# Adding two more key tiles of P on GpSimd before the row sums, and writing the last rows of maxima late in the burst

## The chip, the cores and the metric

The kernel runs on one core of one Trainium2 chip. The metric is device time in microseconds (us), the median of three runs. A profile was taken of one further execution; its times are counted from the start of its span. The engines are called PE (TensorE), DVE (VectorE), ACT (ScalarE), POOL (GpSimd) and SP (SyncE); PEld is the loading of PE's stationary operand.

## What is computed

The reference is an attention whose mask comes from a clustering of queries and keys, followed by two blocks of dense layers:

```
mask   = argmax(q_n . c_n)[:, :, :, None] == argmax(k_n . c_n)[:, :, None, :]
scores = where(mask, scale * q @ k.T, -1e9);  scores -= max(scores)
attn   = exp(scores);  attn /= (sum(attn) + 1e-9)
x      = attn @ v                                   # 2 batches, 8 heads, 768 rows, 64 wide
u      = x + (w_tok_r @ (x cos(x w_theta)) + w_tok_i @ (x sin(x w_theta)))
x      = u + relu(u @ w_ch)
u      = x + (x.T @ U @ V).T
out    = u + relu(u @ w_ch1) @ w_ch2
```

The change touches the attention alone: the sum of `attn` over the keys, and the place of a step that brings the row maxima into the operand of the scores.

## The kernel before

The attention works on 8 groups (`g` = 0 to 7), each two heads (`h` = 0, 1) of one batch. The scores are kept transposed: P, the exponentials, has keys on the partitions, in 6 key tiles of 128 keys by 768 queries in single precision (`pt[g, h, kt]`). Every engine works through its own queue in the order in which the program issues; nothing is reordered between instructions of one engine. That order is written out by hand in `attention()`: a loop over groups, and in it a loop over 6 slots, `p` = 0 to 5.

A slot of a middle group does this, in this order of the program:

- `scores_pair` (L304, L309): the scores of two key tiles by PE, their exponentials by ACT. Head 0 has slots 0 to 2, head 1 slots 3 to 5.
- `max_pair` (L251, L255): the plain scores of two query tiles of the next group by PE, their maxima by DVE straight from PSUM. Behind slot 2 and slot 5, `max_join` takes the last maximum (DVE, L260) and `max_split` splits it into two bf16 parts on POOL: a cast (L271) and a subtraction (L272).
- `join_keys` (L332) adds key tiles 0 and 1 of P into a tile `pj`. In groups 0 to 3 POOL does it (slots 1 and 4), in groups 4 to 6 DVE (slots 2 and 4). `join_third` (L340) adds key tile 2 on POOL, in groups 1 to 3 (slots 2 and 5).
- `split_half` (slots 0 and 1) has POOL subtractions L193; `row_sums` of the group before (end of slot 2) has a DVE reciprocal (L367) and eight small POOL copies (L373).
- `fill` runs background work whose costs the program keeps account of: parts of the clustering (`assign_items`, L124 to L152), the normalisation of the group before (`spread` L379, `norm_x` L383, DVE), and the conversion of weights (`Convert`: ACT L407 and L419, DVE L410 and L414, POOL L423).

Slot 5 of groups 1 to 6 ends in what is called the burst here: the clustering's `sims`, the rows of maxima of head 0 for the next group (`max_rows`: six small PE matmuls L282 of the split maxima, and two ACT copies L285 into the operand `qp`), about 9.6 us worth of background work, the products P times V (`pv`, L317, each of 8 PE instructions) and, between them, the rows of maxima of head 1, and at the end `sum_keys` (L354): matmuls of ones with each tile that is left, which sum P over the keys. In groups 1 to 5 twelve `pv` stand in the burst, in group 6 six (the other six go into group 7). `sum_keys` has 8 PE instructions for each key tile of both heads, so that adding tiles together beforehand makes it shorter. Its sums go to DVE (L357) and into `row_sums` of the next group.

After the attention come the dense layers (`mixer`), from 227 us to the end.

Of the kernel before, what the change touches and what calls it, by code (L numbers as in the profile page):

```python
# [16 lines left out]
ALU = mybir.AluOpType  # L17
# [7 lines left out]
NG = B * NP  # L25
# [16 lines left out]
def tile_cluster_block(ctx: ExitStack, tc: tile.TileContext, qk, v, cent, wth, wr, wi, wch,  # L42
                       u_in, v_in, w1, w2, cst, out):
    nc = tc.nc
# [7 lines left out]
    def slot(name, dt=F32, shape=None):  # L52
        return sp.tile(shape or [P, S], dt, tag="slot", name=name)
# [5 lines left out]
    def bank(name, keep=None):  # L59
        i = ring.popleft()  # L60
        if keep is None:
            ring.append(i)
        else:
            kept.setdefault(keep, []).append(i)
        return pp.tile([P, 512], F32, tag=f"bank{i}", name=name)
# [34 lines left out]
    def load_raw(g, i):  # L100
        t = slot(f"raw{g}_{i}")
        nc.sync.dma_start(out=t, in_=qk[g // NP, g % NP, i])
        raw[g, i] = t
# [8 lines left out]
    def cols(hf):  # L112
        return slice(hf * HALF, (hf + 1) * HALF)
# [174 lines left out]
    pt, v_t, pvt, xT = {}, {}, {}, {}  # L288

    def load_v(g):  # L290
        t = slot(f"v{g}", F32, [P, NT, P])
        nc.sync.dma_start(out=t, in_=v[g // NP, g % NP])
        v_t[g] = t
# [19 lines left out]
    def pv(g, kt, hf):  # L313
        if kt == 0 and hf == 0:
            pvt[g] = banks("pv", "pv")
        for r in range(0, P, 32):
            nc.tensor.matmul(out=pvt[g][hf][r:r + 32, :HALF], lhsT=v_t[g][:, kt, r:r + 32],  # L317
                             rhs=pt[g, r // 64, kt][:, cols(hf)],
                             start=(kt == 0), stop=(kt == NT - 1))

    def pv_out(g):
        xT[g] = slot(f"xT{g}")
        for hf in range(2):
            nc.scalar.activation(out=xT[g][:, cols(hf)], in_=pvt[g][hf][:, :HALF], func=AF.Copy)
        give("pv")

    rl, lsum, joined = {}, {}, {}
# [4 lines left out]
        eng.tensor_tensor(t, pt[g, h, 0], pt[g, h, 1], op=ALU.add)  # L332
        joined[g, h] = t

    wide = set()

    def join_third(g, h):

        t = joined[g, h]
        nc.gpsimd.tensor_tensor(t, t, pt[g, h, 2], op=ALU.add)  # L340
        wide.add(g)

    def sum_keys(g, a, n=3):

        ps = bank("l")
        x = [[pt[g, h, kt] for kt in range(3 * a, 3 * a + n)] for h in range(2)]
        if (g, 1) in joined and a == 0:
            x = [[joined.pop((g, h)), *x[h][3 if g in wide else 2:]] for h in range(2)]
        n = len(x[0])
        for i in range(n):  # L350
            for h in range(2):
                for hf in range(2):
                    o = 32 * (2 * h + hf)
                    nc.tensor.matmul(out=ps[o:o + 32, :HALF], lhsT=ones, rhs=x[h][i][:, cols(hf)],  # L354
                                     start=(i == 0), stop=(i == n - 1))
        lt = slot("lt")[:, :HALF]
        nc.vector.transpose(lt, ps[:, :HALF])  # L357
        lsum[g, a] = lt
# [76 lines left out]
    def conv_start():  # L435
        while conv_load and len(conv_in) < STAGED:
            c = conv_load.popleft()
            c.load()
            c.at = clock[0]
            conv_in.append(c)  # L440
# [30 lines left out]
    def weigh_in(src, n, dst):  # L471
        return [Convert(src, n, i, keep_split(dst)) for i in range((n + S - 1) // S)]
# [378 lines left out]
    def split_half(g, i):  # L851
        split_hi(g, i)
        split_lo(g, i, nc.gpsimd)
        if i:
            pack(g)

    def attention():


        ORDER = [(0, 0), (0, 2), (0, 4), (1, 0), (1, 2), (1, 4)]  # L860
        BURST = (2, 5)
        pvq = deque()
        held[0] = True

        def next_pv():
            g, kt, hf = pvq.popleft()
            pv(g, kt, hf)
            if kt == NT - 1 and hf:
                pv_out(g)

        for g in range(NG):
            nxt = g + 1 < NG
            if g == 1:
                conv_load.extend(weigh_in(wth, NP * DM, wth_t))
                conv_start()
            if nxt:
                load_v(g + 1)
            if g < 2:
                bg.extend(assign.pop(g + 2))
            if g + 3 < NG:  # L880
                for i in range(2):
                    load_raw(g + 3, i)
            if g == 2:
                tok = [c for p in zip(weigh_in(wr, NT * S, wr_t), weigh_in(wi, NT * S, wi_t)) for c in p]
                conv_load.extend(tok[:6])
                conv_start()
                late = tok[6:]
            if g == 5:
                conv_load.extend(late)
                conv_start()  # L890
            if not nxt:
                for t in range(NP):
                    bg.append((1., lambda t=t: split_x(0, t, nc.gpsimd)))
            order = [(1, 0), None, (1, 2), None, (1, 4), None] if g == 0 else ORDER
            for p in range(NT):
                ready = len(pvq)
                clock[0] = NT * g + p
                if order[p]:
                    h, a = order[p]
                    scores_pair(g, h, a)  # L900
                    if h:
                        pvq.extend((g, kt, hf) for kt in (a, a + 1) for hf in range(2))
                if g == 0 and p < 2:
                    mask_direct(1, p, nc.scalar if p else nc.vector)
                if nxt:
                    max_pair(g + 1, p // 3, 2 * p % 6)
                    if p % 3 == 2:
                        max_join(g + 1, p // 3)

                while conv_after:  # L910
                    conv_after.popleft()()
                if p in ((1, 4) if g < 4 or not nxt else (2, 4)):
                    join_keys(g, p // 4, nc.gpsimd if g < 4 else nc.vector)
                    if 4 <= g < NG - 1 and p == 4:
                        owed[0] -= .95
                if 0 < g < 4 and p in (2, 5):
                    join_third(g, p // 5)
                if p < 2 and g + 2 < NG:
                    split_half(g + 2, p)
                if p == (3 if g < 2 else 2) and g + 2 < NG:  # L920
                    mask_rows(g + 2)
                long = 0 < g < NG - 1 and p == 5
                if long:
                    if g + 3 < NG:
                        (_, sims), *items = assign_items(g + 3)
                        sims()
                        bg.extend(items)
                    max_rows(g + 1, 0)
                if g > 0 and p == 5:
                    bg.appendleft((.95, lambda: norm_x(g - 1)))  # L930
                    bg.appendleft((.97, lambda: spread(g - 1)))
                fill(2.5 if not nxt else .3 if p not in BURST or (g > 1 and p == 2) else 9.6 if g > 1 else 4.8)
                if not nxt:
                    for _ in range(min(ready, (2, 2, 2, 0, 4, 4)[p])):
                        next_pv()
                    if p == 5:
                        sum_keys(g, 0)
                elif long:
                    ready = len(pvq) - (6 if g == NG - 2 else 0)
                    for n in range(ready):  # L940
                        if n == ready // 2:
                            max_rows(g + 1, 1)
                        next_pv()
                    sum_keys(g, 0, NT)
                elif p == 2 and g < 2:
                    if g > 0:
                        max_rows(g, 1)
                        sum_keys(g - 1, 1)
                    for _ in range(min(ready, 6)):
                        next_pv()  # L950
                elif p == 5:
                    max_rows(g + 1, 0)
                    for _ in range(min(ready, 6)):
                        next_pv()
                    sum_keys(g, 0)
                    (_, sims), *assign[g + 3] = assign_items(g + 3)
                    sims()
                if g > 0 and p == 2:
                    row_sums(g - 1)
            while bg:  # L960
                fill(.5)
            while g and conv_after:
                conv_after.popleft()()
        held[0] = False
        while len(pvq) > 1:
            next_pv()
        nc.scalar.activation(out=warm, in_=warm, func=AF.Sin)
        next_pv()
        sum_keys(NG - 1, 1)
# [286 lines left out]
```

## Time and profile before

| | |
|---|---|
| runs | 671.27, 668.59, 669.45 us; median 669.45 us |
| profiled execution | 670.76 us, of which the span of instructions is 669.0 us |
| busy, share of the span | PE 98%, PEld 87%, DVE 69%, ACT 54%, POOL 49% |
| chain that ended last | PE 91%, DVE 5%, POOL 1%, ACT 1% |
| mean granted TensorE clock | 0.994 of full speed |

A matmul's end is modelled in the profile, so PE's busy share is no measure of what it could do; idle time of PE, and what ended it, can be read as it stands. A merged row of the timeline gives start, length, engine, line, operation, tiles (written from read), sizes and count, and in brackets the idle time of the engine ahead of it with what ended that. An instruction's row begins when its engine takes it up, so a row longer than its like holds a wait inside the engine.

### The profile page before, as it was taken

What the parts mean: (1) busy time and instruction counts of PE and PEld (TensorE: products, weight loads), DVE (VectorE), ACT (ScalarE), POOL (GpSimd) and SP (SyncE); (2) the same over time, 40 slices, a digit from 0 to 9 for tenths busy, and PEclk for the clock granted to TensorE, in tenths of its full rate; (3) what the DMA queues carried; (4) which work ended last, traced back from release to release, by engine and by line L of the source; (5) the groups of instructions that cost most, each with busy time, mean ns of one, the idle gap of its engine ahead of it and who ended that gap; (6) DMA issues with size and microseconds to landing.
All of it is one profiled execution on the core that took longest, in us unless ns stands there. A gap on an engine that the chain in (4) does not pass through costs nothing.

```text
span 669.0 us, 11891 instructions
## 1 busy us (share of the span) xinstructions
PE 656.9 (98%) x4535; PEld 579.6 (87%) x4536; DVE 463.8 (69%) x795; ACT 359.1 (54%) x726; POOL 325.7 (49%) x331
## 2 busy tenths in 40 slices
PE   8899999999999999999999999999999999999998
PEld 3566787777665699999999998889999999999997
DVE  6888699897799466457374556769876576766554
ACT  8657487667679454555455446634553444533231
POOL 9445296534329433113233144967766564746221
PEclk9799999999999999999999999999999999999999
DMA  6867677695715111003101221113221122110013
GB/s 201 219 145 249 159 172 233 177 228 157 215 35 169 62 48 33 0 18 99 45 23 33 78 70 43 32 32 95 63 80 51 61 79 79 32 33 1 0 48 142
DMA packets 21786, 62.57 MB, mean 94 GB/s; under 512 B 4224, under 2 KB 7296, under 8 KB 21728
## 3 DMA queue, kind: packets, MB, share of 16 engines
q1 hardware_dynamic: 21728, 61.80, 32.2%
q8 instruction: 36, 0.59, 0.4%
q14 instruction: 22, 0.18, 0.1%
HBM read 40.35 MB, written 3.15 MB: 65 GB/s over the span
## 4 chain that ended last, share of the span: by engine, by line
PE 91%; DVE 5%; POOL 1%; ACT 1%; issue 0%; DMA 0%; SPq 0%; POOLq 0%; DVEq 0%
PE acc L824 17%; PE q L772 15%; PE y L590 15%; PE st L304 9%; PE pv L317 9%; PE h L610 5%; PE th L548 5%; PE smax L251 4%; PE l L354 3%; DVE mx L255 3%; PE g L726 3%; PE acc L745 3%; PE tp L628 1%; PE th L552 1%; PE sims L121 1%; PE h L672 0%
## 5 line engine op out<-in xcount | busy, mean ns | idle before, releaser
L824 PE MATMUL acc<-g,wh 128*128 128x384 f32 x448 | 113.7, 334 | 0.0
L786 POOL TENSOR_TENSOR g<-sum,g 128x384 fp32r<-128x384 f32 x56 | 61.8, 1105 | 83.5 <-ACT g L785 83.5
L255 DVE TENSOR_REDUCE mx<-smax 128x1 f32<-128x512 f32 x144 | 89.0, 679 | 10.9 <-PE smax L251 10.8
L780 DVE TENSOR_TENSOR xT<-acc,xT 128x384 f32<-128x384 f32 x112 | 61.9, 554 | 46.4 <-PE acc L824 46.3
L309 ACT ACTIVATE p<-st 128x512 f32<-128x512 f32 x192 | 80.2, 519 | 24.3 <-PE st L304 23.9
L590 PE MATMUL y<-wh,z 128*128 128x384 f32 x384 | 87.6, 340 | 0.3 <-ACT z L568 0.3
L824 PEld LDWEIGHTS acc<-g,wh 128*128 128x128 f32 x448 | 80.9, 188 | 0.1
L304 PE MATMUL st<-qp,kp 128*128 128x256 f32 (+1 forms) x384 | 80.0, 351 | 0.5 <-ACT qp L285 0.2
L423 POOL TENSOR_TENSOR wl<-cv,wh 128x768 fp32r<-128x768 f32 (+1 forms) x31 | 56.5, 1829 | 40.0 <-ACT wh L419 39.7
L824 PE MATMUL acc<-g,wl 128*128 128x384 f32 x224 | 74.8, 334 | 0.0
L304 PEld LDWEIGHTS st<-qp,kp 128*128 128x128 f32 x384 | 58.6, 193 | 17.4 <-issue 7.2
L784 ACT ACTIVATE sum<-sum 128x384 f32<-128x384 f32 x56 | 29.3, 523 | 82.3 <-DVE sum L780 82.3
L780 DVE TENSOR_TENSOR sum<-q,sum 128x384 f32<-128x384 f32 x98 | 53.0, 553 | 24.4 <-PE q L772 20.8
L590 PEld LDWEIGHTS y<-wh,z 128*128 128x128 f32 x384 | 66.9, 188 | 0.5 <-ACT z L568 0.5
L317 PE MATMUL pv<-p,v 128*32 128x384 f32 x768 | 66.6, 487 | 0.0
L574 POOL TENSOR_TENSOR z<-tht,z 128x256 fp32r<-128x256 f32 x24 | 18.6, 774 | 90.8 <-ACT z L568 90.7
L317 PEld LDWEIGHTS pv<-p,v 128*32 128x32 f32 x768 | 38.9, 110 | 18.7 <-issue 8.5
L414 DVE SCALAR_TENSOR_TENSOR cv<-cv,st 128x768 int32<-128x768 int32 (+3 forms) x47 | 49.3, 1049 | 0.8
L590 PE MATMUL y<-wl,z 128*128 128x384 f32 x192 | 48.8, 335 | 0.0
L251 PE MATMUL smax<-kp,qp 128*128 128x512 f32 x192 | 43.9, 348 | 3.7 <-ACT qp L177 1.2
L193 POOL TENSOR_TENSOR lo<-raw,hi 128x768 fp32r<-128x768 f32 x16 | 29.4, 1840 | 31.9 <-ACT hi L188 21.8
L251 PEld LDWEIGHTS smax<-kp,qp 128*128 128x128 f32 x192 | 33.0, 191 | 13.6 <-issue 2.5
(178 smaller groups left out, 1452.7 us busy)
## 6 DMA issues: line engine op xcount, KB each, us to landing
st<-in_w_dram SPq DMA_DIRECT2D x17, 512.0 KB, 3.6
st<-in_w_dram SPq DMA_DIRECT2D x10, 768.0 KB, 4.2
raw<-in_qk_dram SPq DMA_DIRECT2D x16, 384.0 KB, 5.1
qp<-hi SPq DMA_DIRECT2D x26, 192.0 KB, 3.7
st<-in_wr_dram SPq DMA_DIRECT2D x6, 768.0 KB, 4.3
st<-in_wi_dram SPq DMA_DIRECT2D x6, 768.0 KB, 5.3
kp<-hi SPq DMA_DIRECT2D x32, 96.0 KB, 3.3
qp<-lo SPq DMA_DIRECT2D x32, 96.0 KB, 3.1
```

Of the source, the lines that this page charges most:

```text
L251: nc.tensor.matmul(out=ps[:, c:c + w], lhsT=qp[s, h, 0][:, (a + j) * P:(a + j + 1) * P], rhs=kp[s, h, 0][:, k0:k0 + w], start=True, stop=True)
L255: nc.vector.tensor_reduce(mx_t[g, h][:, o:o + n], ps.rearrange("p (n w) -> p n w", n=n), axis=AX.X, op=ALU.max)
L304: nc.tensor.matmul(out=ps[:, c:c + n], lhsT=kp[s, h, w][:, (a + j) * P:(a + j + 1) * P], rhs=qp[s, h, w][:, q0:q0 + n], start=(w == 0), st ...
L309: nc.scalar.activation(out=pt[g, h, a + j][:, q0:q0 + n], in_=ps[:, c:c + n], func=AF.Exp, scale=float(D) ** -0.5)
L317: nc.tensor.matmul(out=pvt[g][hf][r:r + 32, :HALF], lhsT=v_t[g][:, kt, r:r + 32], rhs=pt[g, r // 64, kt][:, cols(hf)], start=(kt == 0), st ...
L414: nc.vector.scalar_tensor_tensor(t, t, 3, self.lw, op0=ALU.logical_shift_left, op1=ALU.bitwise_or)
L423: nc.gpsimd.tensor_tensor(t[:, :c.w], c.t, f32(c.hi[:, :c.w]), op=ALU.subtract)
L590: nc.tensor.matmul(out=yps[u, j][hf][:, :HALF], lhsT=lhs, rhs=w[st][e][:, hf * HALF:(hf + 1) * HALF], start=(st == 0 and n == 0), stop=(st ...
L772: nc.tensor.matmul(out=ps[:, :HALF], lhsT=w[a][:, j * P:(j + 1) * P], rhs=u_block(self.b, y, e, j), start=(n == 0), stop=(n == 5))
L780: nc.vector.tensor_tensor(out, ps[:, :HALF], x, op=ALU.add)
L786: nc.gpsimd.tensor_tensor(t[:, 1], r, f32(t[:, 0]), op=ALU.subtract)
L824: nc.tensor.matmul(out=ps[:, :HALF], lhsT=wv[a], rhs=self.g[i, hf][:, x], start=(m == 0), stop=(m == 5))
```

## The change

In groups 2 to 6 POOL adds key tiles 2 and 3 of P, one after the other, onto `pj`, the sum of tiles 0 and 1: head 0's at slot 3, head 1's at the very start of slot 5. In group 1 `join_third` goes away and nothing takes its place; in groups 2 and 3 the new additions take the place of `join_third`. `sum_keys` then has `pj` and tiles 2 to 5 in group 1 (before: `pj`, 3, 4, 5), and `pj`, 4, 5 in groups 2 to 6 (before: `pj`, 3, 4, 5 in groups 2 and 3, `pj`, 2 to 5 in groups 4 to 6). The rows of maxima of head 1 are written ahead of the last `pv` of the burst, the twelfth or, in group 6, the sixth; before it was in the middle, ahead of the seventh or the fourth.

```diff
-    wide = set()
+    wide = {}
-    def join_third(g, h):
+    def join_more(g, h, last):
         t = joined[g, h]
-        nc.gpsimd.tensor_tensor(t, t, pt[g, h, 2], op=ALU.add)
-        wide.add(g)
+        for kt in range(2, last + 1):
+            nc.gpsimd.tensor_tensor(t, t, pt[g, h, kt], op=ALU.add)
+        wide[g] = last + 1
...
-            x = [[joined.pop((g, h)), *x[h][3 if g in wide else 2:]] for h in range(2)]
+            x = [[joined.pop((g, h)), *x[h][wide.get(g, 2):]] for h in range(2)]
...
                 clock[0] = NT * g + p
+                if 1 < g < NG - 1 and p == 5:
+                    join_more(g, 1, 3)
                 if order[p]:
...
-                if 0 < g < 4 and p in (2, 5):
-                    join_third(g, p // 5)
+                if 1 < g < NG - 1 and p == 3:
+                    join_more(g, 0, 3)
...
                     for n in range(ready):
-                        if n == ready // 2:
+                        if n == min(16, ready - 1):
                             max_rows(g + 1, 1)
                         next_pv()
```

## Rows read from the trace of the kernel before

**Rows 1.** The page, part 4: shares of the chain that ended last, by engine.
```profile
PE 91%; DVE 5%; POOL 1%; ACT 1%; issue 0%; DMA 0%; SPq 0%; POOLq 0%; DVEq 0%
```

**Rows 2.** Timeline of PE, ends of the bursts of groups 2 to 5 (start, us, ...).
```profile
102.35 0.91 PE L354 MATMUL l<-pj,ones 128*32 128x384 f32 x8
...
105.12 1.68 PE L304 MATMUL st<-qp,kp 128*128 128x512 f32 x8
...
127.28 0.91 PE L354 MATMUL l<-pj,ones 128*32 128x384 f32 x8
...
152.15 0.91 PE L354 MATMUL l<-pj,ones 128*32 128x384 f32 x8
...
176.53 0.90 PE L354 MATMUL l<-pj,ones 128*32 128x384 f32 x8
...
179.94 1.68 PE L304 MATMUL st<-qp,kp 128*128 128x512 f32 x8
```

**Rows 3.** Timeline of PE, head 1's rows of maxima in group 6.
```profile
196.52 0.27 PE L282 MATMUL mrow<-identb,m 128*2 128x128 bf16 x3 [1.26 <-POOL m L272]
```

**Rows 4.** Timeline of POOL, behind head 0's maxima in groups 2 to 6.
```profile
89.91 0.21 POOL L272 TENSOR_TENSOR m<-mx,m 128x6 bf16<-128x6 f32 x1
...
114.97 0.21 POOL L272 TENSOR_TENSOR m<-mx,m 128x6 bf16<-128x6 f32 x1
...
140.02 1.78 POOL L373 COPY rl<-rl 32x12 f32<-32x12 f32 x8 [0.35 <-DVE rl L367]
...
165.07 1.78 POOL L373 COPY rl<-rl 32x12 f32<-32x12 f32 x8
...
189.43 1.78 POOL L373 COPY rl<-rl 32x12 f32<-32x12 f32 x8
```

**Rows 5.** Timelines of DVE and POOL in group 7.
```profile
205.26 2.62 DVE L414 SCALAR_TENSOR_TENSOR cv<-cv,st 128x768 int32<-128x768 int32 x1
...
207.01 2.59 POOL L535 TENSOR_TENSOR xl<-xT,xh 128x768 fp32r<-128x768 f32 x1
...
209.56 2.17 POOL L535 TENSOR_TENSOR xl<-xT,xh 128x768 fp32r<-128x768 f32 x1
```

**Rows 6.** Timelines of POOL, DVE and PE, slot 2 of group 1.
```profile
61.18 1.83 POOL L340 TENSOR_TENSOR pj<-pj,p 128x768 f32<-128x768 f32 x1
...
61.78 1.64 DVE L147 TENSOR_TENSOR eqw<-eqw,mi 128x384 bf16<-128x384 bf16 x1
...
65.03 0.50 PE L251 MATMUL smax<-kp,qp 128*128 128x512 f32 x1 [1.16 <-DVE lt L357]
```

**Rows 7.** Timeline of DVE, slot 4 to the burst of group 6.
```profile
192.81 0.94 DVE L332 TENSOR_TENSOR pj<-p,p 128x768 f32<-128x768 f32 x1
...
195.74 0.97 DVE L379 STREAM_TRANSPOSE rb<-rl 128x768 f32<-128x768 f32 x1
196.74 0.96 DVE L383 TENSOR_TENSOR xT<-xT,rb 128x768 f32<-128x768 f32 x1
197.62 0.55 DVE L410 TENSOR_SCALAR st<-st 128x768 int32<-128x768 int32 x1
198.21 0.96 DVE L414 SCALAR_TENSOR_TENSOR cv<-cv,st 128x768 int32<-128x768 int32 x1
```

**Rows 8.** Timeline of DVE, burst of group 4.
```profile
147.77 0.96 DVE L383 TENSOR_TENSOR xT<-xT,rb 128x768 f32<-128x768 f32 x1
...
149.22 0.56 DVE L132 TENSOR_TENSOR eqw<-s_t,mxc 128x384 bf16<-128x384 f32 x1
149.82 0.36 DVE L138 TENSOR_TENSOR eqw<-eqw,cvals 128x384 bf16<-128x384 bf16 x1
```

**Rows 9.** PE's timeline at 20 us; windows: busy us by engine, clock, DMA.
```profile
20.11 0.49 PE L282 MATMUL mrow<-identb,m 128*2 128x128 bf16 x6 [0.75 <-DVE m L272]
...
19.70:26.50 6.80, 6.11 (x22) 4.64 (x23) 5.62 (x10) 3.12 (x8) 5.29 (x8) 0.50 0.96 209
...
180.00:202.00 22.00, 20.74 (x174) 15.28 (x173) 19.94 (x32) 15.89 (x33) 8.35 (x15) 1.00 0.32 119
```

## The prediction

> **What bounds the kernel now.** First the chain that ended last: 91% of it is PE [rows 1], so a microsecond that PE spends or waits in the attention is a microsecond of the kernel, unless a later wait swallows it. The reader should see there that DVE, POOL and ACT hardly hold the end, and that what counts of them is when they release PE. Next PE's timeline at the ends of the bursts [rows 2], for what a key tile costs and when PE would come to the rows of maxima in their new place. Then PE's wait in group 6 [rows 3]: the kernel already has one place where PE stands still for `max_split` on POOL, 1.26 us. Then POOL's timeline behind slot 2 [rows 4], for the moment from which POOL is free for the new additions; and DVE beside POOL [rows 5, 7, 8], because what the additions meet there decides.
>
> **PE's work.** The row sums of group 2 begin at 102.35 with four tiles and end, where the scores of group 3 begin, at 105.12: 2.77. Those of group 5, with five tiles, take 176.53 to 179.94: 3.41 [rows 2]. The difference is one key tile of both heads, 0.64 us of PE. The change adds one tile in group 1, removes one in each of groups 2 and 3 and two in each of groups 4, 5 and 6: 7 fewer net, 7 x 0.64 = 4.5 us less.
>
> **Group 1 loses `join_third`.** POOL's addition at slot 2 runs from 61.18 to 63.01. DVE's L147 was taken up at 61.78 and lasts 1.64, to 63.42, 0.41 behind POOL's end; a DVE instruction of its width takes 0.56 elsewhere [rows 6, 8]. So DVE stood still for 1.1 us, and the sums' transposition L357 behind it releases PE only at 65.03, after 1.16 idle [rows 6]. Without the addition DVE is 1.1 earlier, and so is PE: a gain of 1.1 us. In the burst of group 1 the addition that goes was followed by nothing that PE waited for: nothing.
>
> **POOL's work.** Before there were 6 such additions, now 20, each 1.83 us [rows 6]: 14 more, 25.6 us. That by itself costs nothing as long as POOL catches up in the burst. But head 1's two additions now stand ahead of head 1's `max_split` in POOL's queue, and PE, in order, waits for that split at `max_rows`. The move of `max_rows` to the last `pv` is what pays for it: five `pv` more in groups 1 to 5, two in group 6, each of which is 8 instructions like those of a key tile, 0.64. Behind `max_rows` on PE stand the last `pv`, the row sums and all of the next group. The two ACT copies of `max_rows` come late with it; I cost them at nothing, since `pv_out` behind them in ACT's queue needs the last `pv` anyway, and their reader is slot 3 of the next group. If that cover were gone, ACT's lateness would show in the next group's exponentials. No DMA moves, and no issue on SP changes its place.
>
> **When does the split come?** From the end of the eight copies L373. In groups 2 and 3 they now follow the subtraction directly, ending at 90.12 + 1.78 = 91.90 and 115.18 + 1.78 = 116.96; in groups 4 to 6 they end, as before, at 141.80, 166.85 and 191.21 [rows 4]. From there POOL has five tensor additions in groups 2 and 3 (two of head 0, head 1's `join_keys`, two of head 1) and four in the others, at 1.82 each, then cast and subtraction, 0.5 (two like the 0.21 of [rows 4], and the hand-over; an estimate).
>
> *Free of DVE* this gives 101.5, 126.6, 149.6, 174.6 and 199.0. PE would come to the rows 0.74 (one `pv`, and an estimated 0.1 for the six small matmuls, which had been ahead) ahead of where its sums begin: 101.6, 126.5, 151.4, 175.8 [rows 2]. In group 6 PE stopped at 196.52 - 1.26 = 195.26 [rows 3], and comes two `pv` later, 196.55. So only group 6 would wait, 2.45, which is 1.2 more than now.
>
> *But POOL isn't free of DVE.* In group 7, L414, 0.96 when alone [rows 7], took 2.62: it was taken up at 205.26 and ended at 207.88. POOL's subtraction taken up at 207.01 lasted 2.59 instead of 1.82 and ended 1.72 behind L414's end [rows 5]. Each waited for the other to finish, in turn. So each such DVE instruction that falls between two POOL instructions makes POOL later by about 2.59 - 1.82 = 0.77 where it is 768 wide, and by 2.17 - 1.82 = 0.35 for L410 [rows 5] and for a 384-wide one; for L138, 0.36 long, I take 0.2. The background work puts them exactly there: in group 6 L332, L383, L410 and L414 follow from 192.81 to 199.2 [rows 7], and in group 4 L383, L132 and L138 from 147.77 [rows 8]. Now POOL is busy over all of it.
>
> The transposition L379, which reads one tile, I take to have no part in it.
>
> So, by group, the split's time, PE's arrival and the wait:
> - Group 2: a join L414 in slot 4, L383, L132, L138: 2.1. 103.6 against 101.6: 2.0.
> - Group 3: L383, L132, L138: 1.3. 127.9 against 126.5: 1.4.
> - Group 4: L332, L383, L132, L138: 2.1. 151.7 against 151.4: 0.3.
> - Group 5 (no clustering left; weights in its place): L332, L383, L414, L410: 2.7. 177.3 against 175.8: 1.5.
> - Group 6: the same four, 2.7. 201.65 against 196.55: 5.1, of which 1.26 is there already: 3.8.
>
> New waits 9.0. Group 1 keeps its split early: no wait. What is late next: DVE ends its burst later, in group 6 by the four turns, but PE is then late as well; I cost it at nothing. If DVE were later than PE, the wait would be at the maxima of slot 0.
>
> **PE's clock.** It was 0.50 of full speed, 1.2 GHz, from 19.70 to 26.50, behind a stretch in which PE had idled 0.75 at the end [rows 9]; it did not fall at the 1.26 of group 6 [rows 3], a stretch that stands at 1.00 [rows 9]. Whether it falls in a wait of 5.1 no row says. From below it costs nothing; from above, half of 6.8 us, 3.4. A wait four times the longest that left it alone is nearer to a fall, and part of the low stretch lies in the wait itself: I take 2.0. The Trainium skill ("TensorE: Matmul & The Clock Gate", Part 1) has it that the throttled state is the default and that activity releases it, an idle engine falling back to 1.2 GHz; by that the fall comes, without it the sum is 2.0 less. The fall at 20 us agrees, though the idle time there was short.
>
> **The sum.** -4.5 - 1.1 + 9.0 + 2.0 = +5.4 us. The profiled execution took 670.76 (span 669.0, 1.8 around it), 1.3 over the median 669.45. It becomes 676.2, and the median 674.9. The dense layers keep PE busy with hardly a wait, so what the attention loses arrives at the end.
>
> **The rivals.**
> 1. *POOL late, the clock stays.* The same waits without 2.0: 672.9. For it: one 1.26 wait without a fall. Against it: 5.1 is much longer.
> 2. *POOL in time (the other side).* The mechanism is the turn-taking in the burst: if DVE's background work falls outside POOL's additions, or POOL starts head 0's additions with its copies out of the way earlier, the split comes at the free times above, and PE waits only in group 6: -4.5 - 1.1 + 1.2 = -4.4, 665.0. It decides from the point where less than about 4 us of the 9 are left. Against it: turns are seen in every place where both engines had such work [rows 5, 6], and the DVE order is fixed.
> 3. *More falls of the clock, or DVE late as well.* The waits of 2.0, 1.4 and 1.5 would be enough too, or the turns in slots 4 and 5 delay the maxima. Two more falls at 2.0 and 1 us of DVE: about 680.
> 4. *The additions do nothing for PE.* That `sum_keys` isn't shorter can't be: its list of tiles is cut by the program.
>
> **How the numbers follow.** Forecast 0.45, rival 1 0.22, rival 2 0.16, rival 3 0.13, anything else 0.04. No change that can be told from none is within 0.5%, 666.1 to 672.8. Slower by more: the forecast, most of whose spread lies above 672.8 (0.40), rival 3, and near half of rival 1 (0.10): 0.63. Faster by more: the better part of rival 2: 0.13. The same: 0.24. The range that leaves out 2 in 10 runs from rival 2 with some of its turns kept, 666.0, to rival 3, 680.0; for the forecast alone it is 672.5 to 678.
>
> **What would show it.** `sum_keys` of 24 PE instructions in groups 2 to 6 and 40 in group 1, at the same pace; PE at slot 2 of group 1 without its idle 1.16; a row of L282 with "<-POOL m L272" in groups 2, 3, 5 and above all 6, with 2.0, 1.4, 1.5 and 5.1; POOL without a gap from L373 to L272 of head 1, with DVE's L383, L132 and L414 of 1.5 to 2.6 among them; and 0.50 in the clock behind group 6. Wrong it would be if POOL's additions kept to 1.82 beside DVE, if group 6's wait were under 3, or if PE's time came back in the next group, DVE being the one it had waited for.

## The result and the profile after

The changed kernel takes 675.48 us (median of 6 runs), the kernel before beside it 670.46 (6 runs): 1.0081 times as long, 95% interval 1.0057 to 1.0104, 5.0 us slower. The forecast was 674.9, slower.

The page of the changed kernel, first the busy time of each engine, then the shares of the chain that ended last:

```profile
PE 654.1 (97%) x4479; PEld 579.9 (86%) x4480; DVE 470.6 (70%) x795; ACT 357.6 (53%) x726; POOL 357.4 (53%) x345
...
PE 80%; POOL 7%; issue 5%; DVE 4%; ACT 2%; DMA 1%; SPq 1%; POOLq 0%; DVEq 0%
```

POOL, 1% of the chain before [rows 1], now holds 7% of it, and PE 80% where it had 91%. The chain passes through POOL where PE waits for it, and follows POOL's queue back from there. Where PE waits, its timeline shows (the bracket is the idle time, with what ended it):

```profile
101.83 0.27 PE L282 MATMUL mrow<-identb,m 128*2 128x128 bf16 x3 [1.58 <-POOL m L272]
...
102.56 0.90 PE L355 MATMUL l<-pj,ones 128*32 128x384 f32 x8
...
127.78 0.27 PE L282 MATMUL mrow<-identb,m 128*2 128x128 bf16 x3 [0.94 <-POOL m L272]
...
176.37 0.27 PE L282 MATMUL mrow<-identb,m 128*2 128x128 bf16 x3 [0.93 <-POOL m L272]
...
200.70 0.37 PE L282 MATMUL mrow<-identb,m 128*2 128x128 bf16 x3 [4.89 <-POOL m L272]
```

These are groups 2, 3, 5 and 6; before, only group 6 had such a row, of 1.26 [rows 3]. Group 4 has none. The row sums are shorter, as they should be: in group 2 from 102.56 to the next scores at 104.67, 2.11 for three tiles, where four took 2.77 [rows 2].

POOL and DVE of the changed kernel around group 6's wait:

```profile
188.70 1.78 POOL L374 COPY rl<-rl 32x12 f32<-32x12 f32 x8
190.56 8.61 POOL L341 TENSOR_TENSOR pj<-pj,p 128x768 f32<-128x768 f32 x4
199.12 0.52 POOL L271 CAST m<-mx 128x6 bf16<-128x6 f32 x1
199.72 0.93 POOL L272 TENSOR_TENSOR m<-mx,m 128x6 bf16<-128x6 f32 x1
```
```profile
195.20 0.97 DVE L380 STREAM_TRANSPOSE rb<-rl 128x768 f32<-128x768 f32 x1
196.20 1.31 DVE L384 TENSOR_TENSOR xT<-xT,rb 128x768 f32<-128x768 f32 x1
197.43 2.15 DVE L411 TENSOR_SCALAR st<-st 128x768 int32<-128x768 int32 x1
199.62 0.96 DVE L415 SCALAR_TENSOR_TENSOR cv<-cv,st 128x768 int32<-128x768 int32 x1
```

POOL has no gap from the copies to the split: four additions in 8.61 instead of 7.3, the subtraction of 0.2 in 0.93. L411, which takes 0.55 alone [rows 7], takes 2.15. The two engines take turns, as in [rows 5]. (The line numbers behind L339 are one higher than before.)

The clock, in windows of the changed kernel (busy us and count by engine, then granted clock, DMA share, GB/s):

```profile
190.00:198.50 8.50, 5.81 (x58) 3.79 (x58) 8.36 (x12) 4.49 (x8) 8.18 (x7) 1.00 0.01 2
198.60:205.30 6.70, 4.60 (x36) 2.70 (x38) 3.86 (x5) 2.43 (x4) 4.24 (x5) 0.50 0.53 155
205.40:212.00 6.60, 6.60 (x57) 3.23 (x49) 4.29 (x4) 5.38 (x12) 4.16 (x3) 1.00 0.20 81
```

It falls to 1.2 GHz while PE is idle and stays there for the last product and nearly all of the row sums of group 6, which end at 205.84.

**The ledger.** Each kernel was profiled once, and executions of kernels that are alike ahead of group 1 come to it up to 3.4 us apart (56.06 to 59.49), so the groups are compared by themselves: the time from the first scores of a group (the L304 behind the row sums) to those of the next; for group 1 from its slot 2 (the L282 at 58.25 and 57.09), for group 7 to the first matmul of the dense layers.

| group, us | 1 | 2 | 3 | 4 | 5 | 6 | 7 | sum |
|---|---|---|---|---|---|---|---|---|
| before | 22.75 | 24.12 | 24.93 | 25.52 | 24.37 | 22.01 | 24.94 | 168.6 |
| changed | 22.30 | 25.29 | 25.95 | 24.33 | 24.25 | 26.63 | 24.96 | 173.7 |
| difference | -0.45 | +1.17 | +1.02 | -1.19 | -0.12 | +4.62 | +0.02 | +5.1 |

What follows, the dense layers, takes 442.1 in both. So nothing is given back or lost there, and 5.1 of the ledger is the 5.0 of the medians.

### The profile page after: what moved, and what is told of

It is laid out like the page before. It is cut to its first block, busy times and chain, and to the rows that moved or that the text cites. A ratio compares the mean times of both kernels' runs of the same rounds, so it can differ in the third digit from the quotient of the medians.

```text
span 672.9 us, 11797 instructions
## 1 busy us (share of the span) xinstructions
PE 654.1 (97%) x4479; PEld 579.9 (86%) x4480; DVE 470.6 (70%) x795; ACT 357.6 (53%) x726; POOL 357.4 (53%) x345
## 4 chain that ended last, share of the span: by engine, by line
PE 80%; POOL 7%; issue 5%; DVE 4%; ACT 2%; DMA 1%; SPq 1%; POOLq 0%; DVEq 0%
PE acc L825 17%; PE q L773 15%; PE y L591 15%; PE st L304 6%; PE h L611 5%; PE th L549 5%; PE pv L317 4%; POOL pj L341 4%; PE g L727 3%; PE acc L746 2%; DVE mx L255 2%; PE smax L251 2%; PE l L355 2%; POOL pj L332 1%; PE tp L629 1%
## 5 line engine op out<-in xcount | busy, mean ns | idle before, releaser
L304 PE MATMUL st<-qp,kp 128*128 128x256 f32 (+1 forms) x384 | 79.1, 348 | 0.8 <-ACT qp L285 0.3
L304 PEld LDWEIGHTS st<-qp,kp 128*128 128x128 f32 x384 | 57.8, 191 | 17.5 <-issue 4.9
L317 PE MATMUL pv<-p,v 128*32 128x384 f32 x768 | 68.1, 491 | 0.0
L317 PEld LDWEIGHTS pv<-p,v 128*32 128x32 f32 x768 | 42.9, 110 | 14.6 <-issue 8.5
L415 DVE SCALAR_TENSOR_TENSOR cv<-cv,st 128x768 int32<-128x768 int32 (+3 forms) x47 | 51.1, 1087 | 0.8
L251 PE MATMUL smax<-kp,qp 128*128 128x512 f32 x192 | 44.1, 348 | 2.6 <-ACT qp L177 1.9
L251 PEld LDWEIGHTS smax<-kp,qp 128*128 128x128 f32 x192 | 32.6, 190 | 13.2 <-issue 4.3
```

What stands on the lines that cost most here:

```text
L251: nc.tensor.matmul(out=ps[:, c:c + w], lhsT=qp[s, h, 0][:, (a + j) * P:(a + j + 1) * P], rhs=kp[s, h, 0][:, k0:k0 + w], start=True, stop=True)
L304: nc.tensor.matmul(out=ps[:, c:c + n], lhsT=kp[s, h, w][:, (a + j) * P:(a + j + 1) * P], rhs=qp[s, h, w][:, q0:q0 + n], start=(w == 0), st ...
L415: nc.vector.scalar_tensor_tensor(t, t, 3, self.lw, op0=ALU.logical_shift_left, op1=ALU.bitwise_or)
```

## The experiments

Ten kernels were run; each is set beside runs of the kernel before on the same chip. All diffs are against the changed kernel unless something else is said.

**1. The rows back in the middle.**

```diff
-                        if n == min(16, ready - 1):
+                        if n == ready // 2:
                             max_rows(g + 1, 1)
```

> The changed kernel with the rows of maxima of head 1 back in the middle of the burst; the additions stay. Theory (PE waits for the split behind POOL's additions, and the move hides five products of it): PE comes to the rows 5 x 0.64 = 3.2 us earlier in groups 2 to 5 and 2 x 0.64 = 1.3 earlier in group 6, the split comes when it came, so the waits grow to about 4.8, 4.1, 3.2, 4.1 and 6.2 us: 14 us more, 689.5, and more if PE's clock falls in several of them (up to 697). Rival (PE must wait for the additions anyway, at the row sums, so the place of the rows is of no account): within 1 us of 675.5.

Measured: 695.59 (4 runs) beside 670.27, 1.0377 (1.0349 to 1.0405). PE's waits, groups 2 to 6:

```profile
104.06 0.37 PE L282 MATMUL mrow<-identb,m 128*2 128x128 bf16 x3 [4.79 <-POOL m L272]
...
134.88 0.37 PE L282 MATMUL mrow<-identb,m 128*2 128x128 bf16 x3 [4.09 <-POOL m L272]
...
164.84 0.27 PE L282 MATMUL mrow<-identb,m 128*2 128x128 bf16 x3 [3.06 <-POOL m L272]
...
192.31 0.37 PE L282 MATMUL mrow<-identb,m 128*2 128x128 bf16 x3 [4.14 <-POOL m L272]
...
222.61 0.37 PE L282 MATMUL mrow<-identb,m 128*2 128x128 bf16 x3 [6.18 <-POOL m L272]
```

Each grew by the products that had stood ahead of it, within 0.2 of what was expected. The late rows hide 14 us of POOL's lateness. The rest of the 20 us is in the main the clock: it is at 0.50 behind four of the five waits, and stays up behind the shortest. In groups 2, 3 and 5, where a fall came that the changed kernel doesn't have, the group grew by 2.5, 1.7 and 2.7 more than its wait; in group 4, without one, by 0.1. The windows of groups 3 and 4:

```profile
133.10:139.80 6.70, 4.92 (x38) 3.08 (x42) 5.08 (x7) 0.97 (x2) 1.64 (x3) 0.50 0.33 100
161.70:171.00 9.30, 6.24 (x81) 3.58 (x79) 5.95 (x9) 2.68 (x5) 3.58 (x4) 1.00 0.34 107
```

**2. The late rows alone**, against the kernel before:

```diff
-                        if n == ready // 2:
+                        if n == min(16, ready - 1):
```

> The kernel before with the late rows of maxima alone, no further additions. Theory: the wait of 1.26 us in group 6 goes and nothing else changes: 669.2 beside 670.5 before, in the profile no idle time ahead of L282. Rival (late rows make ACT late for the next group's exponentials, or head 1's scores late): 671 to 674, with PE waiting for ACT in the slots behind a burst.

Measured: 669.35 (12 runs) beside 670.27, 0.9982 (0.9970 to 0.9995). Group 6 takes 20.70 instead of 22.01, PE has no idle time ahead of L282 any more, and the other groups stand within 0.03 of before. The move costs nothing and is worth its 1.3 (0.9 in the medians).

**3. The split ahead of the additions.**

```diff
-                if 1 < g < NG - 1 and p == 5:
-                    join_more(g, 1, 3)
...
                         max_join(g + 1, p // 3)
+                if 1 < g < NG - 1 and p == 5:
+                    join_more(g, 1, 3)
```

> The changed kernel with head 1's additions issued behind the split of its maxima instead of ahead of it; the same work on every engine. Theory (queue order on POOL is what PE waits for): no idle time ahead of L282; the additions end 0.5 us later than now and PE waits for them at the row sums L355 instead, 0.7 in group 2, 0.1 in group 3, 3.1 in group 6: 8.3 us of waits become 3.9. 671.1 if the clock still falls in group 6, 668.8 if not. Rival (PE is held by POOL's total work, whatever the order): the waits only change their place, 675 or more.

Measured: 676.18 (6 runs) beside 670.27, 1.0079 (1.0059 to 1.0099). There is no wait ahead of L282, but the expectation failed: the loss is as large as in the changed kernel, as the rival had it. The rival's reason, POOL's total work, is not all of it, as PE's new waits show:

```profile
185.60 1.60 PE L304 MATMUL st<-qp,kp 128*128 128x256 f32 x6 [2.64 <-DVE lt L358]
...
206.21 0.52 PE L355 MATMUL l<-pj,ones 128*32 128x384 f32 x2 [2.63 <-POOL pj L341]
```

The second was expected (3.1). The first was not, and DVE's timeline in the stretch before it tells where it comes from:

```profile
176.25 2.58 DVE L415 SCALAR_TENSOR_TENSOR cv<-cv,st 128x768 int32<-128x768 int32 x1
...
180.32 2.24 DVE L411 TENSOR_SCALAR st<-st 128x768 int32<-128x768 int32 x1
182.67 2.38 DVE L415 SCALAR_TENSOR_TENSOR cv<-cv,st 128x768 int32<-128x768 int32 x1
184.97 0.57 DVE L358 STREAM_TRANSPOSE lt<-l 128x384 f32<-128x384 f32 x1
```

L415 takes 0.96 and L411 0.55 when alone [rows 7]. Held first by the additions, then by POOL's weight subtractions, DVE comes to the transposition of group 5's sums at 184.97; their PSUM bank is the one that PE needs for the scores of slot 1. The clock fell behind it as well (0.50 from 187.4 to 190.8). With PE no longer held by the split, DVE's lateness is what holds it.

**4. That place again, without group 5's additions.** Against experiment 3, in both conditions:

```diff
-                if 1 < g < NG - 1 and p == 5:
+                if 1 < g < NG - 1 and g != 5 and p == 5:
```

> The kernel with head 1's additions behind the split, without any addition in group 5. Theory (in group 5 the additions hold DVE's weight conversion, the transposed sums L358 come late and PE waits for their bank in slot 1 of group 6): the wait of 2.6 us there and the fall of the clock behind it go, group 5 takes 24.3 and group 6 24 us instead of 28.1; about 3 us less than with them, 673. Rival (that wait comes from the additions of other groups or from a late transfer): it stays, 676 or more.

Measured: 671.72 (10 runs) beside 670.47, 1.0022 (1.0011 to 1.0034). No wait for L358; group 5 takes 24.38 and group 6 24.18 (23.23 and 28.14 in experiment 3), 2.8 less together. The medians lie 4.5 apart; the 1.7 beyond the two groups isn't explained by them, and the profiled execution lost no clock ahead of group 1, which others do.

**5. No new additions in group 6.**

```diff
-                if 1 < g < NG - 1 and p == 5:
+                if 1 < g < NG - 2 and p == 5:
...
-                if 1 < g < NG - 1 and p == 3:
+                if 1 < g < NG - 2 and p == 3:
```

> The changed kernel without the new additions in group 6 alone. Theory: group 6 gives back the 4.6 us that it lost, and the late rows also take the 1.26 that it waited before: 669.6; clock 1.00 over the whole of groups 6 and 7, waits in groups 2, 3 and 5 as they are (1.6, 0.9, 0.9). Rival (the shorter waits add up to the loss, group 6's is a part only): above 672.

Measured: 669.62 (12 runs) beside 670.27, 0.9989 (0.9976 to 1.0002). Group 6 takes 20.73 instead of 26.63, with no wait and no fall of the clock; groups 1 to 5 stand as in the changed kernel (22.30, 25.29, 25.91, 24.31, 24.27), with waits of 1.58, 0.91 and 0.94. So it is group 6 that makes the change a loss: without its additions the kernel can't be told from the one before.

**6. PE kept at work in group 6's wait.**

```diff
-    def max_rows(g, h):
+    def max_rows(g, h, heat=0):
...
+        for _ in range(heat):
+            nc.tensor.matmul(out=ps[:, :P], lhsT=identb, rhs=identb, start=True, stop=True)
...
-                            max_rows(g + 1, 1)
+                            max_rows(g + 1, 1, 80 if g == NG - 2 else 0)
```

> The changed kernel with 80 matmuls of the identity by itself (128 columns, bf16) put on PE in group 6 ahead of head 1's rows of maxima, in the time in which PE stands idle now. Their result is overwritten. Theory (the fall of the clock is caused by the idle time and costs 2.3 us behind it): the split comes when it came, the idle time ahead of L282 is under 1 us, the clock stays at 1.00 and the kernel takes 673.2. Rival (the clock falls for another reason, or the fall costs nothing because another engine bounds group 7): 675.5 and no difference behind group 6.

Measured: 674.47 (5 runs) beside 669.91, 1.0063 (1.0048 to 1.0077). PE's timeline and its window (L282 is L284 here):

```profile
197.80 4.64 PE L281 MATMUL mrow<-identb 128*128 128x128 bf16 x80
202.76 0.27 PE L284 MATMUL mrow<-identb,m 128*2 128x128 bf16 x3 [0.31 <-POOL m L272]
```
```profile
197.80:206.00 8.20, 7.89 (x122) 6.31 (x121) 6.94 (x8) 2.43 (x4) 5.81 (x5) 1.00 0.28 93
```

The split comes no earlier, the clock stays at 1.00, and group 6 takes 24.35 instead of 26.63: the fall cost 2.28 us. The other groups are within 0.02 of the changed kernel's. The medians moved by less, from 675.48 to 674.47, or from 5.0 to 4.6 over the runs of the kernel before beside them, where 673.2 was expected; why they moved by less is open. The 2.28 is the ledger's, from one profile of each kernel.

**7. No normalisation on DVE** in the bursts of groups 2 to 6:

```diff
-                    bg.appendleft((.95, lambda: norm_x(g - 1)))
+                    bg.appendleft((.95, (lambda: None) if 1 < g < NG - 1 else lambda: norm_x(g - 1)))
```

> The changed kernel without the normalisation L384 on DVE in the bursts of groups 2 to 6 (these groups' attention leaves undivided by its row sums); everything else as it is. Theory (POOL and DVE take turns, each DVE instruction with two inputs from SBUF that falls among POOL's additions makes the split 0.7 us later): one of the additions of head 1 shortens from about 2.4 to 1.85 in each group and the waits ahead of L282 fall by 0.7 each: 0.9, 0.2, 0.2 and 4.2 us in groups 2, 3, 5, 6. Rival (an addition takes what it takes, whatever DVE does): additions and waits as they are, 1.6, 0.9, 0.9 and 4.9.

Measured, a single run: 672.05. PE's waits in groups 2, 3, 5 and 6:

```profile
101.04 0.27 PE L282 MATMUL mrow<-identb,m 128*2 128x128 bf16 x3 [0.77 <-POOL m L272]
...
126.36 0.27 PE L282 MATMUL mrow<-identb,m 128*2 128x128 bf16 x3 [0.33 <-POOL m L272]
...
175.03 0.27 PE L282 MATMUL mrow<-identb,m 128*2 128x128 bf16 x3 [1.12 <-POOL m L272]
...
198.82 0.37 PE L282 MATMUL mrow<-identb,m 128*2 128x128 bf16 x3 [4.35 <-POOL m L272]
```

In groups 2, 3 and 6 they fell by 0.8, 0.6 and 0.5, which the rival (additions don't care about DVE) can't have. In group 5 the wait rose by 0.2: DVE's next conversion steps moved up into the free place and took their turns there, the last one ahead of the split's subtraction. A turn is saved only if nothing else takes it.

**8. `join_third` back in group 1.**

```diff
+                if g == 1 and p in (2, 5):
+                    join_more(g, p // 5, 2)
```

> The changed kernel with key tile 2 added on POOL again in group 1, as before. Theory: POOL's addition holds DVE's L147 in slot 2 of group 1, L147 takes 1.6 instead of 0.6, and PE waits about 1.1 us for the transposed sums there again, against 0.64 less of PE's work: 0.5 us slower over group 1. Rival (that wait went for another reason): L147 of 0.6 and no wait.

Measured, a single run: 676.81. DVE and PE in slot 2 of group 1:

```profile
62.16 1.65 DVE L147 TENSOR_TENSOR eqw<-eqw,mi 128x384 bf16<-128x384 bf16 x1
...
65.41 0.50 PE L251 MATMUL smax<-kp,qp 128*128 128x512 f32 x1 [1.16 <-DVE lt L358]
```

The wait of [rows 6] is back to the hundredth, and group 1 takes 22.75 again. In the changed kernel the same L147 takes 0.56.

**9. Additions behind the split, `pj` summed last, one tile in group 6.** The edit of experiment 3, and:

```diff
-            x = [[joined.pop((g, h)), *x[h][wide.get(g, 2):]] for h in range(2)]
+            x = [[*x[h][wide.get(g, 2):], joined.pop((g, h))] for h in range(2)]
...
-                    join_more(g, 0, 3)
+                    join_more(g, 0, 3 if g < NG - 2 else 2)
```

(the same for head 1).

> A version made of the parts: head 1's additions behind the split, pj summed last by PE, and only key tile 2 added in group 6; group 1 and the late rows as in the change. Theory: no wait ahead of L282 and none at the row sums in groups 2 to 6; 6 key tiles fewer on PE (3.9 us), the waits of 1.1 in group 1 and 1.26 in group 6 gone: 6.2 under the kernel before, 664.3. Rival (POOL's extra work holds DVE and by it PE in the slots): 667 or more.

Measured: 673.09 (12 runs) beside 669.91, 1.0038 (1.0021 to 1.0055): slower than before, where 664.3 was expected; the rival held. No idle time of PE for POOL is left, but the wait for L358 in group 6 is (2.75), and groups 3 and 4 take 26.39 and 25.62 with PE waiting in their slots. The groups take 170.4 in sum, 8.0 more than the 162.4 that the expectation makes of the ledger (168.6 - 6.2). DVE holds PE, as in experiment 3.

**10. As many additions as there is room for.**

```diff
-                if 1 < g < NG - 1 and p == 5:
+                if g == 4 and p == 5:
...
-                if 1 < g < NG - 1 and p == 3:
+                if g in (2, 3) and p in (2, 5) or g == 5 and p in (3, 5):
+                    join_more(g, p // 5, 2)
+                if g == 4 and p == 3:
```

> As many additions as POOL has room for, by the group ledger of the runs so far: none in group 1, key tile 2 in groups 2, 3 and 5 behind the split of the maxima, key tiles 2 and 3 in group 4 as in the change, none in group 6; late rows of maxima throughout. Theory (a removed tile is worth 0.64 us only where neither PE waits for the split nor DVE falls behind): group 1 0.45 shorter than before, groups 2 and 3 as before, group 4 1.2 shorter, group 5 0.6 shorter, group 6 1.3 shorter: 3.5 us under the kernel before, 666.5. Rival (any addition beside DVE's background work comes back as a wait): 669.3, as the late rows alone.

Measured: 667.00 (6 runs) beside 670.47, 0.9947 (0.9932 to 0.9963): faster than both kernels. The ledger reads 22.30, 24.10, 24.88, 24.34, 23.71, 20.73, 24.91, in sum 165.0, 3.6 under before; each group is within 0.1 of what was expected. PE has no wait over 0.15 us in all of groups 1 to 7.

## Why the prediction was right, point by point

- **PE's work, -4.5.** Right: 2.11 for three tiles and 2.77 for four, 0.66 a tile. Experiment 10 gets group 5's 0.66 where nothing else changes there.
- **Group 1, -1.1 and +0.64.** Right: -0.45, and experiment 8 shows that POOL's addition was the cause.
- **The waits, 2.0, 1.4, 0.3, 1.5 and 5.1.** Right in mechanism and order, each too long by 0.2 to 0.6: 1.58, 0.94, 0, 0.93, 4.89. The mis-sized term is the turn: priced at 0.77, but an addition with a 768-wide DVE instruction in it took 2.40 to 2.50 in groups 4 to 6, 0.6 to 0.7 over 1.83. With two or three such turns ahead of a split that makes 0.3 to 0.5. That PE waits for the split because it stands behind the additions is shown by experiment 3 (split ahead of them, no wait ahead of L282) and, for group 6, by experiment 5; that DVE's turns are part of it by experiment 7. The Trainium skill ("GPSIMD Engine Reference", Specifications) says that POOL shares its SBUF interfaces with VectorE and contends with those of its instructions that have two SBUF inputs or run in a two-port mode; the trace agrees for L384 (two inputs), which was held (1.31), and the transposition L380 (one input), which was not (0.97). L411 has one input and was held too; it would have to be in such a mode, and no run here shows its mode.
- **DVE's lateness at nothing.** This step was wrong, though by little here. Group 3 lost 1.02 where its wait less its tile makes 0.3. In the view of waits PE's weight loads for L251 wait for ACT's exponentials 1.1 us in the changed kernel, which they didn't before. ACT had waited for DVE's L415, and DVE had been held by POOL, in L147 for instance (1.90, where it takes 0.56 alone). From the changed kernel a row of the waits, DVE and ACT at the start of group 3, and ACT in group 5; then ACT in group 3 before:

```profile
PEld smax L251 <- ACT p L309: 1.1, 4, 0.3
...
102.06 1.90 DVE L147 TENSOR_TENSOR eqw<-eqw,mi 128x384 bf16<-128x384 bf16 x1
...
106.17 0.84 ACT L420 ACTIVATE wh<-cv 128x768 fp32r<-128x768 f32 x1 [2.09 <-DVE cv L415]
106.92 1.61 ACT L309 ACTIVATE p<-st 128x512 f32<-128x512 f32 x4
...
155.73 1.64 ACT L309 ACTIVATE p<-st 128x512 f32<-128x512 f32 x4 [0.16 <-PE st L304]
```
```profile
106.27 1.62 ACT L309 ACTIVATE p<-st 128x512 f32<-128x512 f32 x4
```

  The exponentials of group 3 begin 2.25 us behind its first scores (104.67); before it was 1.15 (105.12). In group 5 they begin 0.77 behind them (154.96), as before: there DVE's L415 was over in time. The prediction looked for such a wait at the maxima of slot 0; it came through ACT instead. In experiment 10, where groups 2 and 3 have no more additions than before, group 3 is back at 24.88. Where PE is not held by the split, this lateness grows: in experiment 9, with no idle time for POOL left, the groups take 8.0 more than expected, and PE waits there for DVE and ACT.
- **The clock, +2.0.** Right: it fell, and cost 2.28 (experiment 6). The 2.0 was chosen between 0 and 3.4, so that it came so near is in part luck. What the Trainium skill says of it ("TensorE: Matmul & The Clock Gate", Part 1: an idle engine falls back to 1.2 GHz) holds for the 4.89; for shorter waits see the last section. Rival 1 thereby falls.
- **The sum.** +5.4 forecast, +5.0 measured, by the ledger 5.1. The new waits were 1.9 too long (7.1 instead of 9.0); against that the clock cost 0.3 more, and 1.4 stands in no term, 0.7 of it in group 3. That the sum is so close is in part luck: these errors cancel. Rival 2 would have needed free additions; rival 3's further falls didn't come at waits of 0.9 to 1.6.

What stays open: groups 2, 4 and 5 lost 0.1 to 0.3 each beyond their waits and tiles; where was not followed. How much of group 3's 0.7 comes of the late exponentials, and how much is of that other kind, was not tried by itself.

## What to carry to other kernels

Work moved to an idle engine is free only as far as what stands behind it in that engine's queue can wait; look first for the instruction behind it that the bound engine needs, and count the turns that it will take with its neighbour there. A removed wait shows the next one: a queue order that takes the split out of the way, here, brought DVE's lateness to light. Add such work group by group, as far as a ledger by group shows room, rather than everywhere.

## What the runs showed of the hardware that was not expected

A wait of 2.63 us on PE left the clock at 1.00 once and not another time. In experiment 3 it stayed up over the wait ahead of 206.21; in experiment 4, in the same place, it fell. The windows of the two:

```profile
203.50:209.50 6.00, 3.37 (x29) 1.78 (x28) 5.87 (x6) 1.22 (x2) 3.48 (x3) 1.00 0.14 27
```
```profile
200.00:203.30 3.30, 3.30 (x15) 1.18 (x7) 3.19 (x4) 1.69 (x2) 1.77 (x1) 0.50 0.52 155
```

The other waits on record add to it: the clock fell behind 2.64 us (experiment 3, ahead of 185.60) and stayed up behind 2.75 (experiment 9) and 3.06 (experiment 1). In groups 1 to 7 no wait of 1.58 or less brought a fall, and each idle time of 4.09 or more did. So between 2.6 and 3.1 us these runs don't tell beforehand whether the price of a fall, up to 2.3 us here, has to be paid.
